# A new step order for a fused DeltaNet and MLP kernel, with 47 filler products instead of 25

## The chip, the cores and the metric

The kernel runs on one core of one Trainium2 chip. Its time is device time in microseconds (us), and lower is better. Three runs of the kernel before took 516.92, 519.6 and 520.19 us, so the median is 519.6 us.

The engines are named as in the profile: PE is the matrix engine, PEld its weight loads, DVE the vector engine, ACT the scalar engine, POOL GpSimd, and SP the engine that issues most DMAs.

## The reference

Inputs are `q`, `k`, `v` of shape (4 batches, 8 heads, 768 tokens, 48) and `beta` of shape (4, 8, 768), all float32. For each batch and head a 48x48 state is carried over the tokens:

```python
k_n = k / (norm(k) + 1e-6)
for t in range(768):
    y[t]  = q[t] @ state
    state = state + beta[t] * outer(k_n[t], v[t] - k_n[t] @ state)
```

The eight heads of a token are then joined to `x` of 384 columns, and a block with a residual follows, with weights of 384x1536 and 1536x384:

```python
xn  = (x - mean(x)) / sqrt(var(x) + 1e-6) * g_ln
out = x + maximum(xn @ w_ch1, 0) @ w_ch2
```

## The kernel before

**Tiling.** The 768 tokens are cut into twelve chunks of 64, `c0` to `c11`. A tile holds all 32 pairs of batch and head of one chunk: two batches on each half of the 128 partitions. The first batch of both halves is called group 0 here, the second group 1 (`g` in the code). Within a chunk the recurrence is solved as a triangular system, so a chunk needs the products of its keys with themselves (`G`, line 822), the inverse of a triangular matrix, and then a few products with the state carried from the chunk before: `ks`, `qs`, `u`, `y` and `s` (lines 1036 to 1108). After each chunk the MLP of its 256 rows follows (`m0` to `m11`, lines 1410, 1430, 1452, 1311 and 1527).

**The first stage.** Chunk 0 has nothing to hide behind, so its inverse is made on PE, round by round (`first_inverse`). In round n, PE makes a product E (line 774), DVE puts parts of it into a matrix under a mask (line 779), PE makes a product Z (line 789), and DVE and ACT copy Z back in two layouts (lines 738 and 732) before the next E can start. There are five rounds, and groups 0 and 1 go through them independently. The first matrix of a group comes from its first products (line 698), scaled on DVE (line 746), masked (line 755) and transposed (line 761). The grams of chunks 2 and 3 (`G2` and `G3`, line 822) and the MLP of chunk 0 follow. Chunk 1 and all later pairs of chunks get their inverse from DVE instead, row by row (`rows_inverse`, lines 910 and 917); this is called a solve here. The solve of chunks 2 and 3, `x1`, reads grams that went out to DRAM and came back (`gd` out, `gb` in), and its result goes the same way (`xd`, `xq`) before a transposition (line 973) and the product `e2` (line 984).

**Order.** The kernel builds a list of 3037 numbered steps, each with an engine and the steps that it depends on. Nothing is scheduled at build time: the string `ORDER` is a table of all step numbers, and `Line.emit` issues them in just this order. Each engine runs its own steps in the order of the table, and the framework adds the waits between engines. A single `f` in the table stands for a filler, a product of zeros that nothing reads:

```python
def zeros():
    nc.tensor.matmul(f_[0][:, 256:512], nought, nought[:, 0:1].to_broadcast([128, 256]))
```

It appears at line 1605 of the profile, two PE instructions for each `f`. Three larger products of zeros (`fill`, 128x512, line 620) are steps 79 to 81. All of them read `nought`, which a DVE memset writes (line 423, step 7).

Steps that the text below names by number:

| step | engine | what it is |
|---|---|---|
| 7 | DVE | memset of `nought` |
| 79, 80, 81 | PE | the three `fill` products |
| 85, 86 | PE | transposition of the keys of chunk 0 (line 631) |
| 82 | PE | transposition of beta (line 642) |
| 103, 104 | PE | first products of groups 0 and 1 (line 698) |
| 118, 119, 120 | DVE | scaling, mask and transposition of group 0 (lines 746, 755, 761) |
| 124, 125, 126 | DVE | the same of group 1 |
| 130, 132 | PE | E of round 1, groups 0 and 1 |
| 134, 140 | PE | Z of round 1, groups 0 and 1 |
| 146, 148 | PE | E of round 2, groups 0 and 1 |
| 330 | PE | `G3` |
| 572 | PE | first product of `m0` (line 1410) |
| 476 to 544 | DVE | the solve `x1` |
| 666 | DVE | transposition of the keys of chunk 4 (line 802) |
| 551 | PE | `e2` |

Of the kernel before, what the change touches and what calls it, by code (L numbers as in the profile page):

```python
# [131 lines left out]
57 52 54 58-59 56 65-66 10-13 25 14 0 22 28 43 8 44 9 5 7 53 55 79 6 71 77 72 89 37 96 76 97 90 1-2 86 85 80 88 98  # L132
91 105 92 99 15 26-27 23 16 34-35 29-30 17 36 100 93 101 31 19 94 87 103 82 81 104 84 24 83 18 95 102 20-21 118 32
124 74 73 106-107 78 69 38 119 108 219-220 75 39 109 120 33 125 110-111 70 40 f 130-131 126 112 122 128 121 123 f f
f 132 134 400 113 405 64 63 262 257-258 313 411 256 260-261 263 404 410 259 311 68 322 312 403 310 399 324 323 325
67 409 402 408 398 133 136 135 41 45 62 254 225 129 127 231 137 f 140 145 213 138 211 235 139 144 142 141 f f f 146
143 241 245 f f 148 253 47 46 42 659 49-51 147 150 154-155 153 149 156 661 60-61 246 152 157 151 4 f f f 162-163 236
115 114 242 217 243 159 221 160 227 212 161 223 247 264 663 255 48 222 166-168 158 265-266 170-171 169 f f 164 f f
178 215 116 412 229 117 237 224 165 267-268 179 172 182 206-207 270 269 232 184 271-272 183 174 173 664 248 660 208
273 3 274-275 209 226 238 177 175-176 185 210 186-187 f f f 180 314 316 315 194 317 240 244 214 276 181 188 239  # L140
192-193 191 195 277-278 189 279 198 318-319 201 199-200 190 280-281 216 282 228 283 f 196-197 284 334 326 361 367
320 285-288 335 289-292 202 327 338 366 360 293-299 203-204 233 340 342-343 300 328-329 346 205 f f f f 330-331
347-348 671 218 397 230 396 234 352 336-337 339 353 332 354-355 572 574 673 665 662 341 251 249 573 344 575 358-359
250 345 349-350 576 578 406 362 577 579 301 407 321 333 432 431 309 307 302-303 308 304 473 306 305 471-472 474 788
351 356 363 357 252 658 415 433-434 582 580 598 370 364 581 599 373 435 604 583 605 368 584 610 586 365 413 470 414
611 585 588 416 372 587 475 590 401 787 790 792 789 791 793-794 589 379 417 591 378 592-596 616 600 374 597 602 601
606 418 376 603 608 436 666 369 476-479 481-489 480 490-495 375 496-499 670 675 672 1073 674 677 377 371 676 500
419-420 501 617 607 380 635 609 636 614 391 421 437 502-507 381 508 795 509 439 510-519 424 615 423 612 620 438 384
390 382 425 422 426 429-430 428 427 637 621 440-441 638 385 392 442 639 445 394 386 447 443 520-523 444 524 393
525-527 622-623 667 624 640 383 678 387 668 446 388 613 389 679-680 528 450 529 395 1085 625-626 618 530 451 448 455  # L150
531 456 449 452 532 650 533 457 534 453-454 535-536 651 537 641 627 642-643 628-629 644 796 458 462 645 630 538 652
539-544 653 631 464 460 465 619 646 461 463 459 826 921 1181 784 928 785 925 669 929 681 924 922 684 686 683 685 545
682 786 687 827 797 647 632 798-799 688-691 694 832 830-831 833 828 838 829 693 1087 1075 1077 1074 695-696 654
697-701 634 930 549 547-548 546 633 931-932 702-706 800 707-709 656 710 550 834 839 844-845 836 933 649 934-935 850
1079 1078 1089 1086 1076 853 851-852 466-467 837 551 859 842 835 552-555 1072 1084 556 860-861 840 862 557-558 560
559 711-713 655 714-715 692 716 561 717-728 562 801 863 841 846 802 864 805 854 856 866 927 843 857 855 936 729 565
564 563 566 865 803 807 806 730 810 808 848-849 809 811 815 812 847 731 804 876-877 869-870 732 813 871 937 567 872
814 733 816 734 817 735-736 822 818 886-887 878 820 825 568 823 819 570-571 569 821 824 468 867 858 469 1090 868 883
938-939 873 888-889 874 737 1080 738 941 890-891 940 942 1179 1176 1184 648 1178 1186 923 926 1177 1366 1188 1185
1187 1183 739-740 657 741 875 742-746 879 747-751 892 943 752-757 1365 1190 1189 880 894 881 895-896 944 901-902 897  # L160
903 898-899 946 945 1547 1088 1091 900 882 1092 1096 893 885 884 1081-1082 1191 975 1182 1558 1371 904 977 1093 905
947 978 1094 948 951 761 760 1083 1095 759 758 1097 1100 1373 1098-1099 983 912 906-907 913-915 984 989 916-917 1192
918 990 920 1370 1372 1375 1652 1377 1369 1376 1378 1180 1368 1379 1374 909 919 979 981 995 949-950 953-954 952 956
762 1193 763 1194-1195 982 765 996 980 985 1101 764 767 766 986 1559 972 908 910-911 1001 1004 969 1548 970 976 971
955 957 959 958 1102 1561 1549 1196 1103-1105 1107-1109 1002 1551 1550 1563 1110-1121 987 991 1010-1012 768 988 992
772 993 1003 1007 1122 1013-1015 769 994 770-771 999 1197 1000 1016 1020-1022 997 1027-1028 998 1198 1023-1024
773-775 777 1201 1199 1123 1560 1005-1006 1017 1008 1018 1565 1564 1553 1546 1552 1124-1125 960 974 1126-1135 1009
1019 1224 1034 1562 1136 1037-1040 1025 961 1654 1380 1137 1026 1200 973 1138 1029-1030 1035 1041-1042 1045
1031-1032 962-963 965 1367 964 1655 1658 1660 1662 1844 1664 1845 1139 1046 1381 1047-1048 1033 1043 1554 1049-1050
1052-1053 1225 1044 1228-1229 1226 968 967 778 966 1243 1232 1036 1051 1202 776 1203 1054-1055 1063 779 783 781-782  # L170
780 1056 1064-1065 1057 1066 1140 1382 1384 1383 1141 1204 1206 1142 1207 1205 1143 1058 1144 1244-1245 1233 1236
1234 1067 1237 1068 1239 1230 1247 1145 1385 1211 1235 1208 1146 1212 1147 1238 1209 1069 1248 1386-1387 1249
1240-1241 1227 1251 1266 1252 1059 1250 1242 1148-1149 1213 1210 1150 1214-1215 1388 1267 1231 1651 1070 1659 1846
1661 1275 1060 1246 1389 1216 1566 1151 1263-1264 1253 1256 1260-1261 1254 1262 1152-1153 1280 2047 1285 2035 1555
1257 1556 1271 1255 1154 1265 1268 1276 1269 1272 1155 1258 1156-1158 1270 1159 1273 1567 1277 1286 1281 1287
1160-1161 1259 1568 1278 1162-1164 1288 1165 1279 1289 1274 1166-1170 1062 1071 1657 1663 1219 1217 1220 1218 1557
1061 1222-1223 1221 1569 1650 1171 1573 1282 1390 1290 1303 1313 1291-1292 1314 1293 1304-1307 1315-1318 1308 1665
1309 1850 1574 1572 1571 1849 2141 1174-1175 1173 1653 1172 1294-1295 1297 1413 1296 1298 1301 1300 1299 1319
1283-1284 1666 1320 1310 1338 1330 1339 1420 1311 1302 2037 1312 1667 1106 1575 1321 1656 1327 1322-1323 1340
1331-1335 1341 1324-1325 1414-1415 1576-1577 1336 1345 1342-1343 1326 1417 1346 1328-1329 2036 1337 1570 1347 1418  # L180
1348-1350 1578-1579 1582 1351 1344 1679 1356 1391-1392 1424 1581 1352 1583-1584 1432 2039 1428 1456 2049 1421 1357
1416 1358-1361 1422 1429 1433 1585 1393 1586 1668 1587 1419 1588 1362 1589-1591 1395 1592-1593 1669 1430 1434
1425-1426 2038 1435 1353 1466 1447-1448 1461 2046 2051 1671 1423 1431 1670 1673 1672 1427 1594 1436 1444 1437 1445
1441-1442 1449 1595 1681 1596 1443 1450 1674 1452 1597 1396 1394 1451 1397 1400 1598-1599 1446 1600 1453 1462 1457
1438 1458 1676-1678 1675 1401 1454 1601 1455 1398 1602 1467-1468 1463 1603 1399 1604 1439 1605 1459 1606 1460 1680
1402 1607 1469 1682 1608 1494-1495 1484 1496 1471 1485 1472 1486-1487 1440 1470 1683 1488-1489 1684 1686 1475-1476
1478 1477 1490 1482 1403 1609-1610 1404 1473 1611 1464-1465 1474 2048 2040 1481 1479-1480 1852 1842-1843 1612 1860
1613 1501-1503 1497-1498 1504 1499 1354 1854 1851 1853 1855 1847 1364 1355 1363 2139 1856 2138 2143 1405 1857 1685
1492 1491 1483 1493 1858 1511 1505-1506 1614 1407 2145 1409 2146 2142 1408 1406 2148 2150 2147 2152 2149 1500 1512
1519 1615 1859 1616-1617 1513 1520 1514-1516 1618 1517 1521 2050 2041 1508 1518 1848 2034 1510 1522-1523 1526 1524  # L190
1527-1528 1525 1507 1529-1531 1688 1410 1687 1412 1709 1411 1619 1720 1509 1716 2052 1620 1689 1691 1532 1692
1696-1697 1690 1693 1621-1625 1698 2042 1694 1537 1871 1861 1713 1865 1862 1864 1863 1538 1710-1712 1539-1540 1714
# [1560 lines left out]
```

## Time and profile before

One execution was profiled. The page gives its span, from the first to the last instruction, and not its whole time.

| quantity | value |
|---|---|
| runs, median of 3 | 519.6 us (516.92 to 520.19) |
| span of the profiled execution | 514.1 us |
| span below the median of the runs | 5.5 us |
| PE busy | 493.1 us, 96% of the span |
| first and last PE instruction | starts at 4.37 us, ends at 510.33 us |
| first product of `m0` | starts at 58.02 us |
| DVE, POOL, ACT busy | 353.5, 284.8 and 206.9 us |
| products of zeros at line 1605 | 50 instructions, from 15.5 to 53.2 us |

A busy PE is not a PE at its peak, since the ends of matmuls are modelled and instructions overlap; the distance from one start to the next is the better price of one. A bracket at the end of a line of the trace tells how long the engine was idle before it and what ended the wait; "issue" there means that nothing the profile shows ended it.

### The profile page before, as it was taken

To read this page: it belongs to the slowest core of one execution; us is meant where nothing else is said; L and a number is where in the kernel's file an instruction comes from. 1 tells how busy PE (TensorE), PEld (TensorE's weight loads), DVE (VectorE), ACT (ScalarE), POOL (GpSimd) and SP (SyncE) were. 2 spreads that over 40 slices of the span, in tenths; PEclk is the share of its full clock that TensorE was granted. 3 is DMA by queue.
4 is the path that set the end of the run, shared out by engine and by line. 5 is a ranking of instruction groups with operands and counts; after the bars stand their busy time and mean duration, and the time that the engine had idled before them with its cause. 6 is when DMAs were issued, how large, how long until landed. Compare 5 with 4: busy or idle time off the path is not lost.

```text
span 514.1 us, 22905 instructions
## 1 busy us (share of the span) xinstructions
PE 493.1 (96%) x10022; PEld 450.7 (88%) x10022; DVE 353.5 (69%) x816; ACT 206.9 (40%) x462; POOL 284.8 (55%) x447
## 2 busy tenths in 40 slices
PE   5897899999999999999999999999999999999997
PEld 3675797668888898999999999999999999999996
DVE  4688479899994999975997847898727346254241
ACT  4785764422533333351434343423514425324140
POOL 2634583144658879749477465283274551844644
PEclk9999999999999999999999999999999999999999
DMA  8958895577338755387454474313660321202011
GB/s 207 251 83 192 221 191 127 128 173 117 67 60 207 123 117 92 73 221 123 80 108 62 105 203 76 99 15 53 132 149 12 88 36 41 57 13 82 8 24 31
DMA packets 181635, 54.56 MB, mean 106 GB/s; under 512 B 164888, under 2 KB 177312, under 8 KB 181536
## 3 DMA queue, kind: packets, MB, share of 16 engines
q1 hardware_dynamic: 168512, 40.10, 37.4%
q10 hardware_dynamic: 10816, 9.83, 6.3%
q0 software_dynamic: 2208, 3.17, 4.3%
q8 instruction: 78, 1.28, 1.1%
q14 instruction: 21, 0.17, 0.1%
HBM read 36.30 MB, written 16.78 MB: 103 GB/s over the span
## 4 chain that ended last, share of the span: by engine, by line
PE 85%; DVE 5%; DMA 3%; issue 2%; ACT 1%; SPq 1%; POOL 1%; DVEq 0%; ACTq 0%; POOLq 0%
PE f L1527 28%; PE f L1311 24%; PE f L1430 6%; PE two L822 3%; PE f L1452 3%; DMA tb<-in_q_dram 2%; PE by L1098 2%; PE by L1036 2%; PE two L1091 2%; PE two L1036 2%; PE two L1108 2%; PE f L1605 1%; DVE xb L917 1%; SPq L404 1%; DMA kr<-in_k_dram 1%
## 5 line engine op out<-in xcount | busy, mean ns | idle before, releaser
L1527 PE MATMUL f<-w_sb,h_all 128*128 128x192 f32 x396 | 83.9, 330 | 0.0
L1514 POOL TENSOR_TENSOR h_all<-h_all 128x256 f32<-128x256 f32 x99 | 74.8, 767 | 9.4 <-PE f L1527 3.3
L1527 PE MATMUL f<-words,h_all 128*128 128x192 f32 x396 | 79.5, 329 | 0.2 <-POOL h_all L1514 0.2
L1552 POOL TENSOR_TENSOR words<-h_all 128x128 f32<-128x128 f32 x66 | 30.2, 478 | 74.4 <-ACT h_all L1338 50.2
L1334 DVE TENSOR_TENSOR h_all<-f,h_all 128x512 f32<-128x512 f32 x72 | 49.2, 686 | 30.5 <-PE f L1311 25.9
L1527 PEld LDWEIGHTS f<-w_sb,h_all 128*128 128x128 f32 x396 | 65.3, 190 | 1.6 <-POOL h_all L1514 0.2
L1527 PEld LDWEIGHTS f<-words,h_all 128*128 128x128 f32 x396 | 65.1, 190 | 1.6 <-POOL h_all L1514 1.0
L910 DVE TENSOR_TENSOR tmp<-xb,gb 128x31 f32<-128x31 f32 (+19 forms) x139 | 56.0, 403 | 3.7 <-POOL xb L897 0.5
L917 DVE TENSOR_TENSOR xb<-xb,tmp 128x31 f32<-128x31 f32 (+19 forms) x139 | 51.4, 370 | 2.5
L1329 ACT COPY h_all<-f 128x512 f32<-128x512 f32 x45 | 25.8, 586 | 62.9 <-PE f L1311 39.3
L404 POOL DMA_DIRECT2D tb<-in_k_dram x64 | 41.9, 658 | 8.2 <-PE f L631 7.1
L1338 ACT ACTIVATE h_all<-h_all 128x512 f32<-128x512 f32 x54 | 32.5, 626 | 30.0 <-DVE h_all L1334 29.8
L1311 PE MATMUL f<-x_new,w_sb 128*128 128x128 f32 x288 | 41.4, 278 | 0.0
L1311 PE MATMUL f<-xnt,w_sb 128*128 128x128 f32 x288 | 40.4, 278 | 0.1
L1311 PEld LDWEIGHTS f<-x_new,w_sb 128*128 128x128 f32 x288 | 37.4, 191 | 0.4
L1311 PEld LDWEIGHTS f<-xnt,w_sb 128*128 128x128 f32 x288 | 36.8, 191 | 0.5 <-issue 0.2
L1430 PE MATMUL f<-xnt,w_sb 128*128 128x256 f32 x144 | 33.9, 383 | 0.0
L1430 PEld LDWEIGHTS f<-xnt,w_sb 128*128 128x128 f32 x144 | 26.7, 190 | 3.5
L605 POOL TENSOR_TENSOR w_sb<-words 128x768 uint32<-128x768 uint32 (+1 forms) x11 | 15.3, 1400 | 23.7 <-issue 18.2
L1545 DVE TENSOR_TENSOR o<-f,x 128x192 f32<-128x192 f32 x33 | 11.2, 348 | 24.9 <-PE f L1527 17.2
L1136 ACT COPY x<-by 128x384 f32<-128x384 f32 x23 | 10.6, 481 | 42.6 <-DVE o L1545 27.2
L1527 PE MATMUL f<-w_sb,words 128*128 128x192 f32 x132 | 27.6, 332 | 0.0
(247 smaller groups left out, 1003.6 us busy)
## 6 DMA issues: line engine op xcount, KB each, us to landing
words<-in_moe_w_ch_dram ACTq DMA_DIRECT2D x20, 384.0 KB, 5.2
gd<-gsb SPq DMA_DIRECT2D x11, 512.0 KB, 4.1
v<-in_v_dram SPq DMA_DIRECT2D x24, 192.0 KB, 3.6
kr<-in_k_dram SPq DMA_DIRECT2D x46, 96.0 KB, 3.7
out_dram<-o SPq DMA_DIRECT2D x46, 96.0 KB, 2.5
xld<-xlt SPq DMA_DIRECT2D x9, 384.0 KB, 3.6
xnt<-xld SPq DMA_DIRECT2D x36, 96.0 KB, 3.0
tb<-in_q_dram SPq DMA_DIRECT2D x40, 64.0 KB, 3.5
```

The lines of the kernel that those rows point to most:

```text
L404: add(eng, cost, lambda: QUEUE[eng].dma_start(out=out_, in_=in_), r, w, bulk=n * ns / 16e3, np=n, **kw)
L910: lambda j=j, n=n, w=w, t=t: nc.vector.tensor_tensor(out=t, in0=xv[:, 0:n, j : j + 1].to_broadcast([128, n, w]), in1=gv[:, j : j + 1, j + ...
L917: "DVE", dve(n * w), lambda t=t, rest=rest: nc.vector.tensor_tensor(out=rest, in0=rest, in1=t, op=ALU.subtract),
L1036: nc.tensor.matmul(dst[half(e), hp, j], src[drows(hp), (e if n else key_half(c, hp, e)) * GP + j], s_all[drows(hp), e, j], start=(n == 0 o ...
L1311: nc.tensor.matmul(wide(p[:, f : f + 128]), w[:, f : f + 128], r, start=start and i == 0, stop=True, skip_group_check=True)
L1329: add("ACT", act(512), lambda: nc.scalar.copy(o, p), pk, ok)
L1334: add("DVE", dve(512), lambda: nc.vector.tensor_tensor(out=o, in0=x, in1=y, op=op), [*xk_, *yk], ok)
L1338: add("ACT", act(512), lambda: nc.scalar.activation(o, o, ACTF.Relu, scale=scale), [], ok)
L1430: nc.tensor.matmul(p[:, 0:TOK], w1_sb[:, t, f * 128 : (f + 1) * 128], xnt[:, t], start=(t == 0), stop=(t == KC - 1))
L1514: add(eng, cost, lambda: e.tensor_tensor(out=out_, in0=x, in1=y, op=op), r, w, port=2 if eng == "Pool" else 1, pr=-2)
L1527: lambda f=f, t=start and f == order[0]: nc.tensor.matmul(p[:, 0:D2], lhs(f), rhs[:, f], start=t, stop=(f == order[-1]), skip_group_check=True
L1552: lambda f=f + i: e.tensor_tensor(out=s3[f], in0=one(0, 0)[0](f), in1=one(1, 0)[0](f), op=ALU.subtract),
```

## The change

The steps, their code and the data that they move stay as they are. The string `ORDER` is replaced by another order of the same 3037 steps, on all five engines, and the table has 47 `f` instead of 25. The beginnings of the two tables, which hold most of the first stage:

```diff
 ORDER = """
-57 52 54 58-59 56 65-66 10-13 25 14 0 22 28 43 8 44 9 5 7 53 55 79 6 71 77 72 89 37 96 76 97 90 1-2 86 85 80 88 98
-91 105 92 99 15 26-27 23 16 34-35 29-30 17 36 100 93 101 31 19 94 87 103 82 81 104 84 24 83 18 95 102 20-21 118 32
-124 74 73 106-107 78 69 38 119 108 219-220 75 39 109 120 33 125 110-111 70 40 f 130-131 126 112 122 128 121 123 f f
-f 132 134 400 113 405 64 63 262 257-258 313 411 256 260-261 263 404 410 259 311 68 322 312 403 310 399 324 323 325
-67 409 402 408 398 133 136 135 41 45 62 254 225 129 127 231 137 f 140 145 213 138 211 235 139 144 142 141 f f f 146
...
+54 52 58 56 59 57 10 66 12 11 13 19 0-1 15 5 49 20-22 14 50-51 8-9 41 43-44 65 7 55 53 6 37 71-72 89 75 96 90-91 76 97
+f f f 79 85-86 80 82 98 77 88 78 38 87 74 105 107 73 84 92 83 23-24 93 35 94-95 34 81 106 104 103 219 108 f 109-110 70
+39 111 69 112 28 99 31 4 26 17 100-102 124 16 18 125 32 3 36 126 29 40 33 2 25 118-119 123 220 120 132 f f f f f f
+130-131 129 121-122 133 113 401 398 63 323 310 258 322 312 400 263 260 64 261 256 259 325 262 257 408 68 313 409 404
+410 311 411 405 403 399 324 67 225 127-128 f 134 137-138 f f f 140 f 135 217 139 145 143-144 241 245 221 47 45 42 46
...
```

Read engine by engine, the first stage changes in these places. On PE the three first instructions are now zeros, ahead of `fill` 79. Steps 104 and 132 (group 1) now stand ahead of 103 and 130 (group 0), and six zeros stand between 132 and 130. On DVE, group 1 (124, 125, 126) comes ahead of group 0 (118, 119, 120). From round 2 on group 0 is first again. Up to step 572 PE has the same set of other steps in both tables, 47 of them, so all 25 and all 47 zeros lie ahead of the first product of `m0`.

## Prediction

> **What bounds the kernel now.** I read the busy times first, then a table of busy time by stretch, then the PE timeline of the first stage.
>
> ```profile
> PE 493.1 (96%) x10022; PEld 450.7 (88%) x10022; DVE 353.5 (69%) x816; ACT 206.9 (40%) x462; POOL 284.8 (55%) x447
> ```
>
> PE is the bound. The stretches are cut at PE's first instruction, the first E product, the first product of `m0`, 110 us and PE's end (columns: length, then busy time and instructions of PE, PEld, DVE, ACT, POOL, then granted clock, DMA share, GB/s):
>
> ```profile
> 0.00:4.37 4.37, 0.00 (x0) 0.00 (x0) 1.28 (x9) 1.43 (x2) 1.88 (x9) 1.00 0.41 76
> 4.37:16.10 11.73, 10.19 (x160) 6.06 (x160) 7.54 (x39) 6.16 (x15) 1.42 (x4) 1.00 1.07 294
> 16.10:58.02 41.92, 34.91 (x1036) 27.49 (x1035) 28.53 (x80) 30.50 (x75) 22.58 (x33) 1.00 0.79 181
> 58.02:110.00 51.98, 48.77 (x1238) 39.51 (x1236) 42.27 (x94) 27.02 (x59) 22.81 (x24) 1.00 0.69 154
> 110.00:510.33 400.33, 399.19 (x7608) 377.69 (x7600) 273.48 (x595) 141.85 (x314) 236.09 (x379) 1.00 0.42 87
> ```
>
> PE's idle time, length less busy, is 4.37 + 1.54 + 7.01 + 3.21 + 1.14 us, and 3.77 after its last product: 21.0 in all. From 110 us on there is nothing to win but 1.14. So the time is, nearly, the start of `m0` plus a fixed load of PE work, and the change is decided before 58.02 us. There the 7.01 us of idle stand beside products of zeros:
>
> ```profile
> 15.47 0.70 PE L1605 MATMUL f<-u 128*128 128x256 f32 x2
> 16.10 0.69 PE L774 MATMUL two<-qt,gsb 64*64 64x64 f32 x32
> 16.73 1.57 PE L1605 MATMUL f<-u 128*128 128x256 f32 x6
> 18.32 0.57 PE L774 MATMUL by<-qt,gsb 64*64 64x64 f32 x23
> ...
> 21.05 1.57 PE L1605 MATMUL f<-u 128*128 128x256 f32 x6
> 23.41 0.69 PE L774 MATMUL two<-qt,gsb 64*64 64x64 f32 x32 [0.78 <-ACT xt L732]
> 24.03 1.14 PE L1605 MATMUL f<-u 128*128 128x256 f32 x4
> 25.10 0.69 PE L774 MATMUL by<-qt,gsb 64*64 64x64 f32 x32
> ```
>
> The reader sees that zeros fill the pause before an E product, and that only what is left over is a wait (0.78 us for ACT's copies).
>
> **The change, part by part.**
>
> *22 more zeros.* Start to start, one alone takes 0.63 us (15.47 to 16.10), two 1.07 (24.03 to 25.10), four 1.94 (51.61 to 53.55). So a run of n costs 0.19 + 0.44 n. Before there are 25 in 11 runs: 13.1 us. After there are 44 in 20 runs behind the first three: 23.2 us. That is 10.1 us more in PE's queue, and PE runs its queue in order: a zero whose pause is over makes the next real product late.
>
> *The first three zeros.* They stand ahead of `fill` 79 and of the transpositions 85 and 86, by which ACT gets the keys. PE is slow there: the first 128x512 product takes 2.08 us (4.37 to 6.45) and the next 1.02 (7.83 to 8.86). Three zeros are 1536 columns with both passes, 3.1 us at the first rate. `fill` 79 then takes 1.0 instead of 2.1, and the transpositions 1.0 (29.73 to 30.76) instead of 1.4 (6.46 to 7.83). Sum: +1.7 us. `nought` comes no earlier: DVE starts about 1.3 us sooner, as POOL makes its first table ahead of two DMA issues (1.36 to 2.57), but eleven DVE steps stand ahead of the memset instead of eight, among them two memsets of 0.27 instead of one. I take no difference; the bounds are -0.5 and +0.5.
>
> *Floor for `m0`.* 10.1 + 1.7 - 8.55 (all idle time from 4.37 to 58.02) = +3.2 us. Less is not to be had from this PE order, even if nothing ever waits.
>
> *Group 1 first.* After 104, DVE scales, masks and transposes group 1 (0.68 + 0.75 + 0.70), with nine small steps between and after (0.1 to 0.3 each) before it gets to group 0. PE reaches 104 at about 13.0 us, the queue's sum behind the three zeros, so 126 ends near 16.8, and 120, behind 2.1 us of its own large steps, one conversion of 0.41 and the small ones, near 19.9. E of group 1 (132) can start at 16.9 instead of 18.32. E of group 0 (130) stands behind it and six zeros (0.62 + 2.83) and starts at 20.1 to 20.4 instead of 16.10. The lead of group 1 is lost at once: its masked copy (133) is behind that of group 0 (131) on DVE. With E of group 0 at 20.2, PE's queue to `m0` holds 34.9 us (busy time before) less 0.62 (132 is past) plus 7.2 (37 zeros in 18 runs, 19.7, less 24 in 10 runs, 12.5): 41.5, so `m0` at 61.7 with no wait at all. Some waits stay: four before 58 us are put down to "issue" (1.56, 0.65, 0.60 and 0.17), which an order cannot be seen to remove. I keep 0.8 of these 3.0, about a quarter, since they came between few zeros and now many zeros cover the pauses. `m0` starts at 62.5: **+4.5 us**. Bounds: the floor +3.2, and +6.7 with all 3.0 kept.
>
> *Behind `m0`.* PE's work is the same. `e2` has 62.3 us of PE products between it and the start of `m0` in both orders (sum of the median distances of each kind). The solve `x1` must be done by then. Its gram `G3` stands 4.47 us ahead of `m0` before (53.55), and in the new queue 3.4 (its own 1.1, products of 0.5 and 0.6, a zero of 0.63, a product of 0.6), so it starts 5.5 later. Step 666 (1.24 us) has moved into the solve on DVE: 38.7 us of DVE work from its first to its last row instead of 37.5. Before, the transposition behind the solve ended at 125.45 and `e2` started at 126.82, which leaves 1.37 of slack. So `e2` can start 5.5 + 1.2 - 1.4 = **5.3 us** later than before; PE alone would bring it 4.5 later, and waits 0.8. Its bounds are 0 and 3 us of waiting (the stretch from 58 to 110 us had 3.21 us idle, which the new order may keep or lose). SP's queue there is reordered too: the DMAs of the first solve and those of `x1` stay mixed, eight and four; I cost that at nothing, since the wait for the gram to land (56.99 to 61.64) covers it.
>
> *The rest.* Step for step the later chunks stand within a few us of PE work of where they were, but for the state products of chunks 2 and 10, which are moved by 9 and 12 us: `qs2` later, `ks10` earlier. Both have their inputs far ahead. Cost 0, bounds -1.1 (all idle time after 110) and +4 (the new order waits as much as the stretch from 58 to 110 did).
>
> Sum: 514.1 + 5.3 = 519.4 us of span. The page gives no time but the span, which lies 5.5 us under the median; I carry these 5.5: **525 us**.
>
> **The rivals.** A change of 1% (5.2 us) is about what a measurement of this kernel can tell from none.
>
> 1. *The zeros fit.* In 16.10 to 58.02 PE's weight loads are busy 27.49 of 41.92 us; if this is PE's true load, 14.4 us are free, and 10.1 more zeros cost nothing. Only the start stays: 519.6 + 1.7 = 521, with 519 to 522 around it. Against it speaks the row of zeros itself: each needs 0.44 us start to start though its two loads take 0.38, and the products beside it wait for the queue. [...] Chance 0.22.
>
> 2. *Faster: products that wait for their weights.* From 110 to 510.33 PE is busy 399.19 us and its loads 377.69. The 21.5 between are products whose weights were not loaded ahead. If the new order halves that, the result is 525 - 10.8 = 514. It decides from 10.5 us saved, about 95 products at the 0.11 by which a product of line 1527 behind another kind (0.43) exceeds one in a row (0.32). Against it: the places where such a product follows its own kind number 376 before and 374 after. Chance 0.05.
>
> 3. *Slower still: the two groups get in each other's way on DVE.* From round 2 on, a copy of group 1 stands behind the masked copy of group 0 that waits for PE behind four zeros (step 141 behind 147). Each such turn costs group 1 the length of a run, 1.1 to 2 us, and it is the later group that ends the stage. If three of the five rounds pay 1.5, `m0` is 4.5 later than forecast, less the 0.8 waited for at `e2`: 529. It decides if the gap between the E products of the groups exceeds 2.2 us (18.32 - 16.10) by round 5. Chance 0.23.
>
> **How the numbers follow.** The forecast has 0.50, with 522.5 to 527.5 around it (the +3.2 and +6.7 of `m0`, with the wait at `e2`). Its own middle lies at the 1% bound, 524.8, so half of it counts as slower. Faster by over 1%: 0.05. Within 1%: 0.25 + 0.22 = 0.47. Slower: 0.25 + 0.23 = 0.48. The range, 519 to 531, leaves out case 2 and the ends of the others.
>
> **What would show it.** In the changed profile the zeros of line 1605 should number 94 and be busy about 26 us; the transpositions of line 631 should start near 8.6 us instead of 6.46; the E product on `two` or `by` of group 0 should start near 20 us; the first product of line 1410 near 62.5; idle PE time before it should be under 3 us, without the first 4.4. `e2` (line 984) should start near 132 with a short wait. The granted clock should read 1.00 throughout, as it did with 25 zeros. The prediction is wrong if line 1410 starts before 60 us, or if PE behind 110 us idles more than 4 us or is busy less than 399.

## The result and the profile after

The changed kernel takes 526.85 us (median of 4 runs, 525.25 to 529.44), the kernel before 518.67 us on the same chip (4 runs, 516.92 to 520.19). The ratio is 1.016, with a 95% interval of 1.0121 to 1.0199: slower by 8.2 us. The experiments below are given as ratios to runs of the kernel before on their own chip, whose medians there were 517.59 to 518.09 us. Slow runs are left out: 526.56 and 976.97 us of the ten of `e1_front_before`, and 831.39 us of the four of `e10_before47`, which is the execution that was profiled (granted clock 0.56 from end to end), so that of this experiment only times are used.

The profiled execution of the changed kernel has a span of 525.2 us, 11.1 more than the one before, and took 526.91 us; in all runs the time around the span is 1.7 to 2.4 us. The lines that answer to those shown of before: first PE's busy time on the page, in which the 44 more instructions of zeros are the only addition.

```profile
PE 504.8 (96%) x10066; PEld 460.2 (88%) x10066; DVE 352.6 (67%) x816; ACT 207.6 (40%) x462; POOL 280.5 (53%) x447
```

The same stretches as before, cut at PE's first instruction, the E product of group 0 (step 130), the first product of `m0`, 110 us and PE's end. Columns: length, then busy time and instructions of PE, PEld, DVE, ACT, POOL, then granted clock, DMA share, GB/s.

```profile
0.00:4.40 4.40, 0.00 (x0) 0.00 (x0) 2.04 (x12) 1.64 (x3) 1.48 (x9) 1.00 0.40 72
4.40:21.80 17.40, 14.22 (x210) 10.23 (x210) 8.91 (x37) 8.80 (x19) 4.31 (x11) 1.00 1.01 285
21.80:63.44 41.64, 39.41 (x1031) 31.12 (x1030) 27.36 (x78) 28.39 (x69) 18.23 (x25) 1.00 0.69 142
63.44:110.00 46.56, 42.86 (x1147) 36.72 (x1141) 33.42 (x75) 25.57 (x58) 22.89 (x25) 0.96 0.68 143
110.00:521.41 411.41, 408.25 (x7688) 382.09 (x7686) 280.46 (x614) 143.25 (x316) 233.59 (x381) 1.00 0.42 88
```

`m0` starts at 63.44 us instead of 58.02, which is 5.42 us of the loss. PE ends at 521.41 instead of 510.33, so 5.66 us more are lost behind `m0`. The granted clock of 0.96 between 63 and 110 us is new: before, it was 1.00 in every stretch.

The first stage in the PE timeline (columns: start, length, engine, line, operation, operands, instructions; the bracket is idle time and what ended it):

```profile
4.41 2.93 PE L1601 MATMUL f<-u 128*128 128x256 f32 x6 [4.41 <-DVE u L419]
7.13 1.33 PE L616 MATMUL f<-u 128*128 128x512 f32 x2
8.30 1.03 PE L627 MATMUL by<-ident,kr 128*128 128x128 f32 x8
9.17 1.03 PE L616 MATMUL f<-u 128*128 128x512 f32 x2
12.49 0.30 PE L638 MATMUL f<-ident,u 16*64 16x8 f32 x8 [2.29 <-DMA u<-in_beta_dram]
...
18.37 0.69 PE L770 MATMUL by<-qt,gsb 64*64 64x64 f32 x32 [0.89 <-DVE qt L757]
18.99 2.88 PE L1601 MATMUL f<-u 128*128 128x256 f32 x12
21.80 0.69 PE L770 MATMUL two<-qt,gsb 64*64 64x64 f32 x32
```

The three zeros, `fill` and the transpositions come as forecast (8.30). Then PE stands for 2.29 us for the DMA of beta (step 65), which POOL issues at 7.12 us instead of 1.36, because eleven other steps stand ahead of it there. E of group 1 is where E of the last group was before (18.37 against 18.32), and E of group 0 comes at 21.80 instead of 16.10.

Behind `m0`, PE's waits by what ended them (columns: us in all, times, longest) and then a stretch of its timeline:

```profile
PE f L980 <- issue: 2.4, 2, 2.0
PE f L1406 <- issue: 1.0, 1, 1.0
PE f L1307 <- DVE h_all L1330: 0.9, 1, 0.9
PE two L1087 <- issue: 0.6, 1, 0.6
PE by L948 <- issue: 0.6, 1, 0.6
```

```profile
85.24 0.82 PE L1406 MATMUL f<-xnt,w_sb 128*128 128x128 f32 x5 [0.98 <-issue]
85.99 1.15 PE L1032 MATMUL two<-s_all,kt 48*64 48x48 f32 x64
87.07 0.70 PE L980 MATMUL f<-xnj,gsb 32*32 32x32 f32 x59
89.79 0.32 PE L980 MATMUL f<-xnj,gsb 32*32 32x32 f32 x5 [2.02 <-issue]
90.04 2.29 PE L1406 MATMUL f<-xnt,w_sb 128*128 128x128 f32 x9
```

The reader sees one step cut in two, 59 of its 64 MATMUL instructions and then, 2.02 us later, the other 5, with no engine or DMA of the data that ended the pause. From 89.66 to 93.07 us the clock record stands at half, and the products at 90.04 us take longer with it: nine in 2.29 us, where eleven took 1.52 from 82.74 us on. The stops share one thing. Count all of PE's instructions from the start, products, weight loads and semaphore instructions together. In the traces of before, after and nine of the experiments (all but `e10_before47` and the two with a tail), 56 of PE's waits of over 0.3 us are put down to "issue". 53 of them stand at the 194th or 195th of a block of 256 instructions, among them seven of the eight of before and all five of after, and these 53 end 1.2 to 1.8 us behind the end of a packet of queue q8. The other three are one pause of 0.60 us, in three kernels, ahead of the same product (line 1072 before). By its counts, q8 carries PE's program:

```profile
q8 instruction: 79, 1.29, 1.1%
```

79 packets of 16 KB for some 20,250 instructions, so 256 to a packet. The rest of this text has two questions: what the front lost, and whether these blocks, and not the order itself, set what is lost behind it.

### The profile page after: what moved, and what is told of

Read it like the earlier page. It is cut to its first block, busy times and chain, and to the rows that moved or that the text cites. A ratio compares the mean times of both kernels' runs of the same rounds, so it can differ in the third digit from the quotient of the medians.

```text
span 525.2 us, 22966 instructions
## 1 busy us (share of the span) xinstructions
PE 504.8 (96%) x10066; PEld 460.2 (88%) x10066; DVE 352.6 (67%) x816; ACT 207.6 (40%) x462; POOL 280.5 (53%) x447
## 4 chain that ended last, share of the span: by engine, by line
PE 80%; DVE 8%; SPq 4%; issue 3%; DMA 2%; ACT 1%; POOL 1%; DVEq 0%; POOLq 0%; ACTq 0%
PE f L1523 27%; PE f L1307 21%; PE f L1426 5%; PE two L818 4%; PE f L1406 4%; SPq L400 4%; PE f L1448 3%; DVE tmp L906 2%; PE two L1032 2%; PE by L1032 2%; PE by L1094 2%; DVE xb L913 2%; PE two L1087 2%; PE two L1104 1%; DMA u<-in_beta_dram 1%
## 5 line engine op out<-in xcount | busy, mean ns | idle before, releaser
L1510 POOL TENSOR_TENSOR h_all<-h_all 128x256 f32<-128x256 f32 x99 | 73.3, 751 | 19.0 <-PE f L1523 9.4
L1523 PE MATMUL f<-w_sb,h_all 128*128 128x192 f32 x396 | 81.7, 331 | 0.0
L400 POOL DMA_DIRECT2D tb<-in_k_dram x64 | 41.7, 656 | 0.7 <-issue 0.3
L1601 PE MATMUL f<-u 128*128 128x256 f32 x94 | 27.0, 415 | 4.4 <-DVE u L419 4.4
L1132 ACT COPY x<-by 128x384 f32<-128x384 f32 x23 | 10.9, 479 | 50.4 <-DVE o L1541 34.3
```

The costliest lines, as they stand in the source:

```text
L400: add(eng, cost, lambda: QUEUE[eng].dma_start(out=out_, in_=in_), r, w, bulk=n * ns / 16e3, np=n, **kw)
L1510: add(eng, cost, lambda: e.tensor_tensor(out=out_, in0=x, in1=y, op=op), r, w, port=2 if eng == "Pool" else 1, pr=-2)
L1523: lambda f=f, t=start and f == order[0]: nc.tensor.matmul(p[:, 0:D2], lhs(f), rhs[:, f], start=t, stop=(f == order[-1]), skip_group_check=True
```

## The experiments

All kernels differ from one of the two in their table alone, if nothing else is said. Zeros feed no output, so leaving them out or adding some leaves the result as it is.

### Half of each table

A step's prerequisites all stand ahead of it in either table, so the two can be joined: one table up to step 572 (`m0`), then the steps that have not been issued, in the order of the other. Five or six steps of engines other than PE, which only the other table has ahead of `m0`, stand directly ahead of step 572.

```diff
 e1_front_before
-ORDER = changed table
+ORDER = table before up to 572 (25 f), then the changed table's remaining steps
 e2_back_before
-ORDER = changed table
+ORDER = changed table up to 572 (47 f), then the table before's remaining steps
```

> All steps up to step 572 (`m0`) stand in the order of the kernel before, with its 25 zeros; all later steps in the order of the changed kernel. The traces put the loss of the changed kernel at +5.4 us at `m0` and +5.7 us behind it. My theory (two separate losses, front and back): `m0` at 58.0, the back's own loss returns, 518.7 + 5.7 = 524.4, range 522 to 526. Rival 1 (the back's idle time and its stretch of halved clock come only because of what the front does, the block of 256 instructions falling elsewhere with 22 zeros fewer): 518.7 to 521. Rival 2 (the back's order loses nothing by itself, the front decides all): 518.7 within 1 us.

> The other half: all steps up to step 572 in the order of the changed kernel, with its 47 zeros; later steps in the order of the kernel before. My theory: `m0` at 63.4, TensorE's idle time behind it as before, 518.7 + 5.4 = 524.1, range 522.5 to 526. Rival 1 (stalls move with the count of zeros, so both halves meet): 526 to 529. Rival 2 (a late front is made good further on, by slack in the solve of `x1`): 518.7 to 521.

Ratios to the kernel before, by front and back:

| | back as before | back as changed |
|---|---|---|
| front as before, 25 zeros | 1 | 1.0096 (1.0056 to 1.0136), 523.09 us |
| front as changed, 47 zeros | 1.0275 (1.0242 to 1.0307), 531.49 us | 1.016 (1.0121 to 1.0199), 526.85 us |

The back alone costs 0.96%, 5.0 us, which lies in the range of the theory. But the theory had `m0` at 58.0 us, and in the profiled execution, the slowest of the eight (524.74 us), it starts at 61.14. Up to there PE has the same instructions as in the kernel before, and so the same block places; the same stop is longer (PE timeline, the kernel before and then `e1_front_before`):

```profile
55.12 0.46 PE L822 MATMUL f<-kt 48*64 48x64 f32 x16 [0.65 <-issue]
57.59 0.46 PE L818 MATMUL f<-kt 48*64 48x64 f32 x16 [2.02 <-issue]
```

Half clock follows the second from 58.71 us on. So a block place tells where a stop can fall; how long it is differs between executions, and how much of the 5.0 us belongs to the back alone stays open.

The other half fell outside of what every theory said: with the back of the kernel before, the changed front costs 14 us, although it brings `m0` at 63.52, where the changed kernel has it. So 8 to 9 us are lost in an order that loses none of them behind its own front. PE's waits in `e2_back_before` from 63.6 us on:

```profile
PE two L1107 <- issue: 2.4, 2, 1.7
PE by L951 <- issue: 2.0, 1, 2.0
PE by L1035 <- issue: 1.7, 1, 1.7
PE f L1409 <- ACT h_all L1417: 1.5, 1, 1.5
PE f L1526 <- DVE o L1544: 0.9, 1, 0.9
PE f L1526 <- issue: 0.7, 1, 0.7
```

6.8 us are "issue" stops; three of them, of 1.7 to 2.0 us, are followed by 3.41 us of half clock each (from 88.7, 184.3 and 204.8 us). What differs for this back is that 22 more zeros, of four instructions each, stand ahead of it: all its blocks of 256 fall 88 instructions earlier in it.

### The places of the blocks

```diff
 e5_split12: kernel before, its last 12 f written h
+if w == "h":
+    self.filler[0](256, 384)
+    self.filler[0](384, 512)
-def zeros():
-    nc.tensor.matmul(f_[0][:, 256:512], nought, nought[:, 0:1].to_broadcast([128, 256]))
+def zeros(at=256, to=512):
+    nc.tensor.matmul(f_[0][:, at:to], nought, nought[:, 0:1].to_broadcast([128, to - at]))

 e6_fewer4: kernel before, four f fewer
-... f f f 132 ... f f f 146 ... f f f 162 ... f f f 180 ...
+... f f 132 ... f f 146 ... f f 162 ... f f 180 ...
```

> The kernel before, with its last 12 products of zeros (31 to 53 us) each split into two of 128 columns: the same columns, the same order, 48 TensorE instructions more ahead of `m0`. The traces so far show TensorE standing still where the 194th of every 256 of its instructions follows sooner than 3.6 to 3.9 us after the 194th of the 256 before. Theory (where these places fall decides how long it stands): with the intervals between the kernel before's own records and all places 48 instructions earlier, pauses behind `m0` grow by 7 to 9 us, and each pause over 1.7 us brings 3.4 us of halved clock: 524 to 529, ratio 1.013 to 1.022. Rival (the places do not matter, the instructions are paid by their own time): 12 more products at under 0.1 us each, in pauses: ratio 0.998 to 1.003.

> The kernel before with 4 of its 25 products of zeros left out (the third ahead of steps 132, 146, 162 and 180; they feed no output): 16 TensorE instructions fewer ahead of `m0`. By the same working the pauses shrink by 2.2 to 2.6 us; the steps behind the zeros had waited 0.05 to 0.15 us for their operand in any case. Theory: 515 to 516.5, ratio 0.995 to 0.998, below the kernel before. Rival 1 (places do not matter): ratio 0.999 to 1.001. Rival 2 (4 products fewer let the clock fall in the first stage): 1.01 or more.

`e5_split12` took 524.86 us, ratio 1.0144 (1.0082 to 1.0206). It has the order and the columns of the kernel before, and its `m0` starts even earlier (56.93 us); 48 instructions more ahead of it cost some 7 us behind it. The same three steps in both, first the kernel before and then `e5_split12` (PE timeline):

```profile
171.75 0.83 PE L984 MATMUL f<-xnj,gsb 32*32 32x32 f32 x64
172.51 1.15 PE L1036 MATMUL two<-s_all,kt 48*64 48x48 f32 x64
173.48 1.11 PE L1036 MATMUL by<-s_all,qt 48*64 48x48 f32 x64
```

```profile
172.25 0.75 PE L987 MATMUL f<-xnj,gsb 32*32 32x32 f32 x64
172.94 1.15 PE L1039 MATMUL two<-s_all,kt 48*64 48x48 f32 x64
173.90 0.99 PE L1039 MATMUL by<-s_all,qt 48*64 48x48 f32 x54
176.66 0.43 PE L1039 MATMUL by<-s_all,qt 48*64 48x48 f32 x10 [1.77 <-issue]
```

The first has no stop, the second one of 1.77 us in the middle of a step, and 3.41 us of half clock from 177.0 us. So the places matter: all four runs (522.56 to 526.43 us) lie above all thirteen of the kernel before on that chip (514.18 to 521.02). `e6_fewer4`, 16 instructions the other way, took 516.85 us, ratio 0.999 (0.9955 to 1.0025): this neither shows the gain of 2.2 us nor excludes it, and it is no kernel that beats the one before. In its trace `m0` starts at 59.35 us, behind a stop of 1.93 us in `G3`, where the kernel before has one of 0.65.

The time from the start of `m0` to PE's end, one profiled execution each, shows what the places do to both backs (`e8_zeros25`, the changed order with 25 zeros, is described below):

| back | 25 zeros ahead of it | 47 zeros ahead of it |
|---|---|---|
| as before | 452.31 us | 462.50 us (`e2_back_before`) |
| as changed | 458.11 us (`e1_front_before`), 455.44 us (`e8_zeros25`) | 457.98 us |

With 25 zeros the back of before is 3.1 to 5.8 us shorter, with 47 it is 4.5 us longer. Neither order is the better one by itself.

### The supply by itself

A tail behind all work of the kernel before, in which nothing waits for an operand and, from 518 us on, no data move:

```diff
+def dense(n):
+    for k in range(n):
+        q = slice(32 * (k % 4), 32 * (k % 4) + 32)
+        nc.tensor.matmul(f_[0][q, 256:288], nought[q, 0:32], nought[q, 0:1].to_broadcast([32, 32]))
+
+def rate():
+    dense(512)
+    for _ in range(24): zeros()
+    for _ in range(8):
+        dense(32)
+        for _ in range(9): zeros()
```

This is `e13_rate4`. `e12_rate` had `dense(256)` first and `q = slice(0, 32)` for every product, so that all lay in one quarter of rows and columns.

> The kernel before with a tail that feeds no output and is not to be counted in its time: 256 fp32 products of 32x32 zeros back to back (1024 TensorE instructions, four blocks of 256), then 24 products of 128x256 zeros, then eight times 32 of the small products followed by 9 of the large. No other transfer runs by then. Theory (TensorE gets 256 instructions in no less than 3.6 us, whatever they do): the 256 small products take 13 to 15 us, standing still at the 194th of every 256, with a stretch of halved clock behind it; 32 of them between large ones take 0.75 us as in the kernel's own steps. Rival (the places of stops in the kernel come of other transfers or of waits for operands): 6 to 7 us for all 256, at 0.023 us each, and no stop.

> The tail again, now with products that outrun the supply in question: in the run before, every small product lay in the same quarter of the array rows and columns and took 64 ns at the full and 106 ns at half clock, so that 256 instructions took 4.1 us or more by themselves. Here four neighbours lie in four different quarters, as in the kernel's own steps (0.75 us for 32 products, 23 ns each). 512 of them back to back (2048 instructions, eight blocks), 24 large products of zeros, then eight times 32 small and 9 large; the tail feeds no output. Theory (256 instructions in no less than 3.6 us): a stop at the 194th of every 256, one every 3.6 to 4.0 us whatever the clock, 28 to 32 us for the 512; 32 between large ones in 0.75 us at the full clock. Rival (no such bound): 12 us at the full clock or at most 24 at half clock, and no stop at those places.

`e12_rate` did not decide: at 64 ns for each product the 256 instructions take 4.1 us by themselves, and no stop was seen. But its clock fell, with PE busy all the time (columns: length, busy time and instructions of PE, granted clock, DMA share, GB/s):

```profile
509.00:513.00 4.00, 4.00 (x108) 1.00 0.36 98
513.00:517.00 4.00, 4.00 (x84) 0.54 0.02 4
517.00:521.00 4.00, 4.00 (x79) 0.50 0.01 4
```

The half clock lasted 27.3 us, until six us after the large products had come back. `e13_rate4` decided (PE timeline; x counts the products' instructions, and each has a weight load beside it, so x128 are 256 instructions):

```profile
514.81 1.32 PE L1611 MATMUL f<-u 32*32 32x32 f32 x125
516.64 1.27 PE L1611 MATMUL f<-u 32*32 32x32 f32 x128 [0.51 <-issue]
520.38 1.93 PE L1611 MATMUL f<-u 32*32 32x32 f32 x128 [2.47 <-issue]
523.85 1.93 PE L1611 MATMUL f<-u 32*32 32x32 f32 x128 [1.54 <-issue]
527.60 1.93 PE L1611 MATMUL f<-u 32*32 32x32 f32 x128 [1.82 <-issue]
...
542.85 0.31 PE L1611 MATMUL f<-u 32*32 32x32 f32 x3 [1.82 <-issue]
543.09 12.73 PE L1606 MATMUL f<-u 128*128 128x256 f32 x48
555.76 0.75 PE L1611 MATMUL f<-u 32*32 32x32 f32 x64
```

PE works 1.3 us (1.9 at half clock) on 256 instructions and then stands, eight times. From one restart to the next it is 3.47 to 4.02 us, mean 3.74, from 519.94 us on at half clock: the 512 products take 28.3 us. Spaced by large ones, 32 take 0.75 us (the last line) and never stop. In this tail a packet of q8 starts 1.1 to 1.7 us after a restart, takes 0.9 to 1.2, and PE goes on 1.3 to 1.5 us behind its end. The three add up to the 3.5 to 4.0, and PE is through its 256 instructions, in 1.3 to 1.9 us, before the packet has landed. In the kernels the packet does not always come so: in the kernel before it starts 3.3 us after the restart at 49.20 us, in `e1_front_before` 4.9 us after the one at 50.29, and a single block can be quicker than 3.5 us behind an early packet (2.02 us, from 351.91 to 353.93 in the kernel before). So the 3.6 to 3.9 us of the expectation for `e5_split12` are no firm bound: the kernel before has no stop at 353.93 us, and one at 54.48, 5.27 us after the restart at 49.20. What decides when a packet starts is not shown.

### The front: zeros, the load of beta, the order of the groups

```diff
 e3_no_zeros: changed table, all 47 f left out
 e8_zeros25: changed table, 22 f left out
-f f f f f f 130 ... f f f 140 ... f f f f f 146 ... f f f f 150 ... f f f f f f 196 ... f f f f 330
+f f f 130 ... f 140 ... f f 146 ... f f 150 ... f f f 196 ... f f 330
 (one fewer ahead of 164; none ahead of 109, 162, 182, 206, 314, 315)
 e10_before47: table before, zeros of the changed table ahead of the same steps
 (the run of six between 130 and 132, three ahead of 79)
```

> The changed kernel with all 47 products of zeros of the table left out (they feed no output), its order otherwise unchanged. My theory as the traces correct it (most zeros lie in waits; the late load of beta and group 1 being first cost the rest): `m0` at 60.0 to 61.5 in place of 63.4, whole 524 to 525.5. Rival 1 (the zeros are the whole loss of the front): `m0` at 58 or earlier, 521 or less. Rival 2 (zeros fit into pauses and cost nothing): `m0` at 63.4, 526.9. Rival 3 (they hold the granted clock up): the clock falls to half in pauses of the first stage, its 128x256 products take 0.85 us in place of 0.44, and the time is 528 or more.

> The changed kernel with 25 products of zeros, as many as before, in place of 47 (22 left out of the runs ahead of steps 130, 140, 146, 150, 164, 196 and 330 and single ones elsewhere; they feed no output). Theory: steps 130, 140, 146, 150 and 164 had their operand 0.7, 1.7, 2.1, 1.0 and 1.0 us before they started, so two to three of these come back on the chain: `m0` 1 to 3 us earlier (60.4 to 62.4); the places of the instruction blocks move by 88, which by the intervals of the changed kernel's own records changes its pauses by less than 1 us; ratio 1.010 to 1.014. Rival 1 (the 22 hold the clock up): the granted clock falls to half in the first stage as in the run without zeros, ratio 1.02 or more. Rival 2 (zeros in the pauses cost nothing): `m0` at 63, ratio 1.016.

> The order of the kernel before with the zeros of the changed kernel: 47 products, each run ahead of the step that it stands ahead of in the change (the run of 6 between the two first E products, so ahead of step 132; three ahead of the first `fill`). It is the second half of the change by itself. Theory: the three at the slow rate put `fill` from 4.4 to 7.1 and, with nothing else late, all transpositions 1.5 to 2.7 us later; the other runs are longer than pauses whose operand came 0.05 to 0.2 us before the step: `m0` at 61 to 63; behind it the instruction blocks fall 88 places earlier, which by the intervals of the kernel before's own records adds 5 to 6 us of standing still and one or two stretches of halved clock: 526 to 531, ratio 1.016 to 1.025. Rival 1 (zeros lie in pauses, blocks do not matter): 0.998 to 1.003. Rival 2 (only the front pays): 521.5 to 523.5, ratio 1.007 to 1.010.

`e3_no_zeros` took 539.1 us, ratio 1.0416 (1.0383 to 1.045). My theory had it the wrong way round, and rival 3 was right: `m0` starts at 67.29 us instead of 60 to 61.5. The granted clock shows why (same columns as the first table of stretches):

```profile
0.00:20.00 20.00, 11.20 (x158) 7.52 (x158) 8.11 (x42) 8.38 (x17) 4.56 (x16) 0.83 0.82 218
20.00:40.00 20.00, 12.43 (x366) 10.75 (x370) 12.71 (x33) 14.32 (x33) 7.31 (x12) 0.53 0.82 149
```

An E product takes 1.13 us there instead of 0.69. So zeros are no idle filler: without them the clock is at half from 10.9 to 17.8 and from 21.2 to 41.7 us. Of the 14.3 us by which this profiled execution is longer than that of the change, 3.9 lie ahead of `m0`. The rest lies behind it, where the blocks fall at other places (188 instructions are missing ahead of them) and the clock is at half in four stretches, so it can't be put down to the pauses that the zeros had filled.

`e8_zeros25` took 526.13 us, ratio 1.017 (1.0112 to 1.0229), no better than 47. Up to step 188 the 22 zeros had indeed been in the way: it starts at 44.84 us instead of 49.05. Then E of round 5 (step 196) waits for DVE:

```profile
51.25 0.69 PE L769 MATMUL by<-qt,gsb 64*64 64x64 f32 x32 [3.09 <-DVE tmp L905]
```

Its operand, step 189, stands on DVE behind six steps of the first solve and a conversion of 2.5 us (step 228), which all stand behind it in the table before; DVE ended it at 51.10, 5.6 us after the end of step 188. In the changed kernel, with the same order on DVE, this takes 3.6 us, since step 228 takes 0.41 us there; why it took 2.5 here is not shown. Behind this pause the clock was at half from 52.3 to 59.1 us, a stop of 0.99 followed at 55 us, and `m0` started at 64.40. What the zeros had cost was taken by this one long step, the clock and the stops.

`e10_before47` took 531.22 us, ratio 1.025 (1.017 to 1.033), at the upper end of the expectation. It is the change's second half alone, and it costs more than the whole change, though the intervals overlap. Beside `e2_back_before`, the other kernel with 47 zeros and the back of before, that is what the shift of blocks would give; its trace can't be used to show the stops.

```diff
 e4_beta_first: changed table, 65 first
-54 52 58 56 59 57 10 66 12 11 13 ... 41 43-44 65 7
+65 54 52 58 56 59 57 10 66 12 11 13 ... 41 43-44 7
 e7_beta_third: changed table, 65 behind 11
-10 66 12 11 13 ... 41 43-44 65 7
+10 66 12 11 65 13 ... 41 43-44 7
 e11_group0: e7_beta_third, and group 0 first
-104 103 ... 100-102 124 16 18 125 32 3 36 126 ... 118-119 123 220 120 132 f f f f f f 130-131 129 121-122 133
+103 104 ... 100-102 118 16 18 119 32 3 36 120 ... 124-125 123 121-122 220 126 f f f 130-131 f f f 132 129 133
```

> The changed kernel with step 65 alone (the DMA of beta that step 82 waits for) put first on POOL, as it stands in the kernel before; nothing else moved. My theory: step 82 starts near 9.2 in place of 12.5, as soon as step 80 is through, `fill` no later than 7.2; group 1 gains all of it, group 0 gains until it meets the zeros: `m0` 2 to 3.3 us earlier (60.1 to 61.4), whole 523.6 to 525. Rival 1 (what stands behind is held by the columns that ACT loads and by the normalisation, so that another wait takes the place of this one): `m0` 0 to 1 us earlier, 526 to 526.9.

> The changed kernel with step 65 (the DMA of beta) on POOL directly behind step 11 and so ahead of the masks 49 to 51 and of `ident` and `eye`; in the run with step 65 in front of everything, `nought` was 0.64 us later and TensorE took 7.1 us instead of 5.8 from the first zero to the end of step 80. Here steps 10 and 11 keep their place. Theory: first zero at 4.4, step 82 at 10.2 to 11.5 in place of 12.5, `m0` at 61.2 to 62.5, ratio 1.010 to 1.014. Rival (what is won at step 82 is lost at group 0, which waits for the columns and stands behind group 1): `m0` at 63, ratio 1.015 to 1.017.

> The changed kernel with step 65 behind step 11 as in the last run of that kind, and group 0 first: 103 ahead of 104 on TensorE, 118 to 120 ahead of 124 to 126 on DVE, 130 ahead of 132, with three of the six zeros ahead of each. Zeros stay 47. Theory (the order of the groups cost the rest of the front): 130 at 16.0 to 16.6, 132 at 18.3 to 19.0, `m0` at 59 to 60.5 in place of 61.1; behind `m0` the loss of the back stays, partly larger by longer stops for instruction blocks: ratio 1.008 to 1.013. Rival 1 (it does not matter which group is first): `m0` at 61.1, ratio 1.013 to 1.015. Rival 2 (what the front wins is lost again at the stops between 78 and 92 us and in the solve of `x1`): `m0` at 59 to 60.5, but ratio 1.013 to 1.016.

| kernel | first zero | step 82 | 130 | 132 | `m0` | ratio |
|---|---|---|---|---|---|---|
| changed | 4.41 | 12.49 | 21.80 | 18.37 | 63.44 | 1.016 (1.0121 to 1.0199) |
| `e4_beta_first` | 5.05 | 12.14 | 21.46 | 18.02 | 63.09 | 1.0144 (1.0118 to 1.0171) |
| `e7_beta_third` | 4.41 | 10.14 | 19.46 | 16.03 | 61.09 | 1.0142 (1.0086 to 1.0197) |
| `e11_group0` | 4.41 | 11.21 | 17.64 | 19.87 | 61.24 | 1.0108 (1.0033 to 1.0184) |

With step 65 first, `nought` is 0.64 us later, and step 82 no longer waits for beta, but PE reaches it only at 12.14 us. The clock shows why: its record starts at 7.74 us in the changed kernel and at 11.18 here, and ahead of it products take about twice as long (the first `fill` 1.91 us, the next 1.02). This start differs between executions with the same front, too (7.44 us in the kernel before, 10.92 in `e1_front_before`), so `e4_beta_first` does not show what an early load of beta is worth, and its whole time of 524.51 us, which lies in the range of the theory, does not confirm it.

With step 65 behind step 11 the record starts at 7.76 us, and `m0` comes 2.35 us earlier, as expected: the late load of beta is 2.3 of the 5.4 us. Between 78 and 90 us PE then stands for 1.2, 1.8 and 1.8 us at three block places, and the clock is at half for 6.8 us instead of 3.4. Even so it takes 457.95 us from the start of `m0` to PE's end, as in the changed kernel (457.98), so this execution keeps the whole gain (PE ends at 519.04 instead of 521.41). The ratios, 1.0142 and 1.016, can't tell such a gain from none.

`e11_group0` has `m0` at 61.24 us instead of 61.09, and I had expected 59 to 60.5. That does not mean that the order of the groups cost nothing: the clock record starts at 9.94 us here, the first `fill` and the transpositions take 1.91 and 1.58 us instead of 1.34 and 1.03, and step 82 comes 1.07 us later. From step 82 to Z of group 0 (134) it takes 10.11 us instead of 11.03, so having group 0 first is worth 0.9 us. It is not more because E of group 0 is 1.8 us earlier, but its masked copy 131 is still behind the six large DVE steps of both groups; in the table before, 131 stands ahead of 126. The whole time is the lowest of the four, though the intervals overlap.

## Why the prediction came out as it did

The time, 526.85, lies in the range of 519 to 531 and 1.9 us over the forecast; it is slower by over 1%, which had a chance of 0.48. That it came so near is luck: the sum under it was wrong in two terms that nearly cancel. The span grew by 11.1 us, not by 5.3. And the 5.5 us that were carried as the distance of the span from the median are mostly not there in other runs, where 1.7 to 2.4 us lie around the span: the profiled execution of before was a quick one.

- **22 more zeros** (+10.1 us in the queue): right in size, line 1601 is busy 27.0 us with 94 instructions. Right too that they delay real products, by 4.2 us at step 188 (`e8_zeros25`). But taking them away did not bring `m0` earlier there, and the sum had no term for what zeros do for the clock, which without any is at half for 27 of the first 42 us (`e3_no_zeros`).
- **The first three zeros** (+1.7): the transpositions came at 8.30, as forecast, but they were not on the path. The load of beta was, by 2.3 us (`e7_beta_third`). The prediction had counted the queue of PE and not that of POOL, in which step 65 now stands behind eleven others.
- **`nought`** at 4.19 to 4.35 instead of 4.15 to 4.32: as forecast.
- **Group 1 first**: 132 was forecast at 16.9 and came at 18.37, 130 at 20.1 to 20.4 and came at 21.80, both late by the load of beta: without it they come at 16.03 and 19.46 (`e7_beta_third`). That group 1's lead is lost at once on DVE was right; the order of the groups is worth 0.9 us (`e11_group0`).
- **Start of `m0`** (+4.5, bounds +3.2 to +6.7): +5.42. PE was idle 5.41 us between its first instruction and `m0`, not under 3; 2.29 of it was the load of beta. Without the late load `m0` is 3.07 us later than before (`e7_beta_third`), just under the floor. So this term, too, came near by luck: an estimate that was 1.4 too high stood against a wait of 2.3 that was missing. How these 3.07 us divide between the zeros and the order is not shown, but for the 0.9 of the groups.
- **`G3` and `e2`** (+5.5 and +5.3): +6.29 and +6.58. The wait of `e2` for the solve, 0.8 us in the sum, did not come. The transposition behind the solve ends at 132.75 us, PE has products without a pause of 0.15 us or more from 89.79 us on, and `e2` (line 980) follows the last of them:

```profile
132.05 0.70 DVE L969 STREAM_TRANSPOSE xnj<-xt 128x512 f32<-128x512 f32 x1
132.32 1.15 PE L1032 MATMUL by<-s_all,qt 48*64 48x48 f32 x64
133.40 0.72 PE L980 MATMUL f<-xnj,gsb 32*32 32x32 f32 x60
```

  So PE alone brought it 6.58 us later: the 5.42 of `m0`, and 1.16 from there to `e2`, where the stops and the half clock lie. The solve, too, took longer than forecast, 42.8 us from its first step to step 544 instead of 40.3, not +1.2 but +2.5. DVE waits in it for 4.7 us, against 1.9 before: 3.2 of it for ACT, which had itself waited until 101.81 us for products of PE (line 1056), and 0.6 for PE's products of chunk 1 (step 443 ends at 105.41, and step 444 starts at 105.48). All these products stand in PE's queue behind the stops of 80 to 90 us.
- **The rest** (0, bounds -1.1 to +4): this is the term that failed. PE ends 11.08 us later, so 4.5 us are lost behind `e2`'s 6.6. Of the 5.66 us behind `m0`, 2.5 are idle time of PE (6.86 instead of 4.35 us): "issue" stops 4.6 instead of 3.8, and waits for other engines 2.1 instead of 0.4, of which 1.7 are for DVE at lines 1307 and 1523. The other 3.15 are longer busy time for the same work, of which the 3.41 us of half clock make up to 1.7. Some 1.5 us are spread thinner than I can assign, and I did not test them apart from the rest of the back.
- **Granted clock 1.00 throughout**: wrong, it was 0.96 from 63 to 110 us. And the 1.00 of the first 7.4 us before and 7.7 us after is read from no record: products take about twice their time there (a 128x512 product 2.08 us before, against 1.02 later; the three zeros 2.93 us after, against 2.88 for six from 18.99 us on).
- **Rival 1** (the zeros fit, 519 to 522) is out by the time, and step 188, 4.2 us earlier with 22 zeros fewer, shows that they did not fit. (47 zeros in the old order cost 2.5%, but that has the shift of the blocks in it.) The headroom read from the weight loads, 14.4 us, was not there. **Rival 2** did not come: PE's busy time less its loads' behind 110 us is 26.2 us instead of 21.5. That all of this is products whose weights were not loaded ahead is not shown either: before, 3.5 us of it are pauses of the loads at line 1430, whose products take 0.22 us from start to start and their loads 0.19. **Rival 3** did not decide. Its test was badly chosen: the E products of the groups are 5.1 us apart in round 5, over the 2.2 that it named, but they were 5.7 apart before; they are further apart than before in round 2, by 3.8 instead of 1.7 us, and by 0.5 us in rounds 3 and 4.

## What to carry to other kernels

A table of steps that is ordered by waits and durations alone misses PE's stops at the block places: in `e13_rate4` small products one after the other took 3.47 to 4.02 us for every 256 instructions, and 32 of them between large ones 0.75 us without a stop. Any instruction added early in the program moves all later blocks, and 48 of them cost 1.4% in `e5_split12`, so compare two orders only at several shifts of the blocks, or the shift is measured for the order. Before two traces of a first stage are compared, look where the record of the clock starts in each (7.44 to 11.18 us here). And before fillers are judged by the pause they stand in, look at the granted clock without them (half for 27 of the first 42 us in `e3_no_zeros`).

## What the runs showed of the hardware

**PE's stops stand at one place of each 256 instructions, and 256 quick ones took 3.5 to 4.0 us.** `e13_rate4` shows the time with nothing else at work (3.47 to 4.02 us from one restart to the next), and `e5_split12` that 48 instructions of shift cost 1.4%. Queue q8 moved 79 packets of 16 KB for some 20,250 PE instructions of the changed kernel, and 53 of the 56 "issue" stops end 1.2 to 1.8 us behind the end of such a packet. Among the small products of `e13_rate4` a stop took up to 2.47 us, and among its 128x256 products, from 543.09 us on, none is seen. In the changed kernel, where the large products of the MLP stand between the small ones, no "issue" stop of over 0.3 us comes after 140.53 us.

**The clock falls to half without PE being idle for long.** After stops of 1.7 to 2.0 us between small products the record shows 3.41 us of half clock (`e2_back_before`, `e5_split12`, the changed kernel), and in `e12_rate` it fell 3.5 us after PE began on 32x32 products, with no idle time at all. In the changed kernel, too, PE had no pause over 2.3 us behind its first instruction. So the clock fell here without a longer pause; how little work it takes was not measured. At the start, the record of full clock begins at 7.44 to 11.18 us in the traces used here, and ahead of it a 128x512 product takes up to 2.08 us instead of 1.02.

**The spread of the runs goes with these stretches.** Of 13 runs of the kernel before on one chip, the three with a mean granted clock of 0.999 took 514.18 to 515.58 us, and the five at 0.990 to 0.993 took 518.09 to 521.02. One stretch of 3.41 us at half clock lowers the mean of a 515 us run by 0.0033.
